# x^T of the fourth chunk by way of memory, and a first load without a fill in front of it

## The chip, the cores and the metric

The kernel runs on one core of one Trainium2 chip. A core has five engines that each work through a queue of their own: PE (TensorE, matmul), DVE (VectorE), ACT (ScalarE), POOL (GpSimd) and SP (SyncE), which here issues every DMA. Engines wait for each other by semaphores. The metric is the device time of one launch in microseconds (us). The kernel before takes 489.73 us, the median of 4 runs (489.62 to 489.83).

## The reference

Two blocks follow each other, all in fp32. The first is a gated recurrence over 4 batches x 8 heads, with sequence 768 and head size 48:

```
f = 1 / (1 + exp(-f_logit))
for t in range(S):
    state = f[t] * state + outer(k[t], v[t])      # per batch and head, 48 x 48
    y[t] = q[t] @ state
```

The outputs y are laid side by side by head as x, 3072 tokens x 384. The second block is a multiplicative feed-forward: `a = x @ w1`, `b = x @ w2`, `h = (a * b) @ w3`, `out = h @ w_out`, with 1024 inner columns. The weights come as 64-bit floats and are turned into fp32 on the chip.

## The kernel before

The 3072 tokens are cut into 24 chunks of 128 (NU = 24; u is the chunk, six per batch). A chunk of the recurrence is done as a small attention. Its gates come from f_logit by a sigmoid on ACT (L385), a forward scan and a backward scan over the gates on DVE (L393, L415) give the factors by which q and k are scaled (L409, L424), and PE makes the products inside the chunk (`pairs`), turns K (`turn`), applies the values (`values`), adds what the state gives (`from_state`) and updates the state (`update`). q, k and f of a chunk lie in tiles of 112 partitions: one head of each pair in partitions 0 to 47, the other in 64 to 111. Partitions 48 to 63 are a gap, which `setup` fills (30.0 for f, 0.0 for q and k): it fills partitions 32 to 63, and the loads then overwrite 32 to 47. So the first load of each such tile waits for its fill. In the kernel before all these fills are on POOL.

Four chunks make a block of 512 tokens (n is the block, NB = 6). The feed-forward wants x transposed, xt, in a tile of 128 x 3 x 512. How the y of a chunk gets there depends on the chunk:

- For u below NPE (= 4), PE does it: ACT brings y from PSUM (L663), six matmuls with a permutation (`moved`, L692) turn it, and ACT copies the result into xt (`settled`, L697).
- For the others, SP writes ys to a scratch tensor yt in memory (`written`, L684, two DMAs of 96 KB) and reads it back in its new order (`gathered`, L687, one DMA of 192 KB).

The constant NPE also chooses other things for the first four chunks, such as how the products are laid out in PSUM.

In block 0 the feed-forward is plain. `part(0, 2)` multiplies the tokens of chunks 0 and 1 by the first half of w1 and w2: four groups for a, then four for b, each of three fp32 matmuls of 256 columns. `part(2, 4)` does the same for chunks 2 and 3, then come groups of 512 columns for the second half of the weights. All are at L714, from the helper `three`. ACT takes each a out of PSUM (L751) and DVE multiplies b onto it (L756). Four PSUM banks serve the groups. From block 1 on the products are done with seven multiplications in place of eight (Strassen's way, in Winograd's form).

Beside that the weights are prepared. For each piece, ACT makes two passes over the 64-bit words (L1112, L1115), and DVE four (L1118, L1119, L1123, L1129). w3 and w_out are folded into one matrix on PE (L1176, eight folds), each fold as soon as its piece of w3 is done.

The order of instructions on each engine is made when the kernel is built: the class `Plan` lists tasks with an estimated cost, priorities and dependencies, and always takes the task that can start first. Engines then run that order strictly, and only waits shift it in time. A task that is removed or gets another cost therefore moves its neighbours on all engines, SP's queue among them. In the built program each DMA has one of eight completion semaphores in turn, and so a DMA is issued only after the one eight places before it has landed.

Of the kernel before, what the change touches and what calls it, by code (L numbers as in the profile page):

```python
# [44 lines left out]
B, H, S, D = 4, 8, 768, 48  # L45
# [13 lines left out]
NLEAF = 6  # L59
NQ = HP * C  # L60
NPE = 4
NRAW = 3
NF = 4
DH = DM // 2
# [125 lines left out]
def rows(par):  # L190
    return slice(64 * par, 64 * par + D)


def heads_of(u):

    return range(HP) if u < NPE else (0, 2, 1, 3)


def side(u, hp, par):

    if u < NPE:
        return par, hp
# [4 lines left out]
def ranged(ctx, tc, q, k, f_logit, v, w1, w2, w3, w_out, out, ident, w12, wc, left):  # L207

    nc = tc.nc
# [17 lines left out]
    qs, ks, fs = ([keep.tile([R, NQ], F32, name=f"{nm}{i}") for i in range(n)] for nm, n in (("q", 3), ("k", 2), ("f", 2)))  # L227
# [10 lines left out]
    def at(a, *shape):  # L238
        n = 1
        for m in shape:  # L240
            n *= m
        t = place[:, a : a + n]
        return t.rearrange("p (a b) -> p a b", a=shape[0]) if len(shape) == 2 else t
# [37 lines left out]
    def heads(t):  # L281
        return t.rearrange("p (h c) -> p h c", c=C)

    def setup():
        nc.scalar.activation(warm, nc.const_aps.tensor(0.0, (R, 1), F32), AF.Sigmoid)
        for i in range(2):
            nc.gpsimd.memset(fs[i][32:64], 30.0)
            nc.gpsimd.memset(ks[i][32:64], 0.0)
            nc.gpsimd.memset(qs[i][32:64], 0.0)
            if i == 0:  # L290
                make_identity(nc, ident)
        nc.gpsimd.memset(early[32:64, 2:4], 30.0)
        nc.gpsimd.memset(early[32:64, 0:2], 0.0)
        nc.gpsimd.memset(qs[2][32:64], 0.0)
        nc.gpsimd.memset(qs[3][32:64], 0.0)
        nc.vector.memset(floor, FLOOR)
        nc.vector.memset(heads(floor)[:, :, 0], 1.0)
        nc.vector.memset(back, 0.0)
        for t in gate:
            nc.vector.memset(t[:, NQ : NQ + 1], 0.0)  # L300
        for t in sb:
            nc.vector.memset(t, 0.0)

        nc.gpsimd.memset(perm, 0.0)
        for i, (kc, hp) in enumerate(met):
            for par in range(2):
                for r, t, at_, n in runs(2 * hp + par):
                    if t == kc:
                        a = 64 * par + at_
                        nc.gpsimd.tensor_copy(perm[:, i, r : r + n], ident[0:R, a : a + n])  # L310

    def runs(h):

        at_ = 0
        while at_ < D:
            t, r = divmod(h * D + at_, P)
            n = min(D - at_, P - r)
            yield r, t, at_, n
            at_ += n
# [7 lines left out]
    def need(u):  # L327
        return (0.0, 1.0, 2.0, 3.0)[u] if u < 4 else 60 + 14.5 * (u - 4)

    def past(u, n, *names):  # L330
        return [tk[u - n][nm] for nm in names if u >= n and nm in tk[u - n]]

    def moves(n, size, rate, emit, deps, prio, late=0.0):


        for j in range(n):
            i = plan.add("SP", 0.45, (lambda: None) if j else emit, [d] if j else deps, prio - j * 1e-3, takes=["lane"], lag=0.6)
            d = i
            t = plan.add("DMA", size / n / rate, lambda: None, [i], prio - j * 1e-3, lag=1.3 + late, frees=[i])
        return t  # L340

    def loaded(dst, u):

        if u < NPE:
            nc.sync.dma_start(dst, v[u])
# [6 lines left out]
    def front(u):  # L352

        s, t = st[u], tk[u]
        n0 = need(u)

        def load(dst, src):
            def emit():
                for par in range(2):
                    nc.sync.dma_start(dst[rows(par)], src[u, par])  # L360
            return emit

        fu, qu, ku = (x[u if u < 4 else u % n] for x, n in ((fs, 2), (qs, 3), (ks, 2)))

        def free(n, *names):

            if u < 4:
                return []
            return asked[8:9] + [tk[u - n if u - n >= 4 else u % n][nm] for nm in names]

        t["lf"] = moves(2, 197, 250, load(fu, f_logit), free(2, "g"), n0 - 30)
        t["lk"] = moves(2, 197, 250, load(ku, k), free(2, "k"), n0 - 29.5)
        t["lq"] = moves(2, 197, 250, load(qu, q), free(3, "q"), n0 - 29)

        def load_v():
            s["v"] = at(12288 + NQ, DM) if u == 3 else loads.tile([P, DM], F32, name="vt")
            loaded(s["v"], u)

        t["lv"] = moves(
            1 if u < NPE else 3, 197, 320, load_v, [] if u == 3 else past(u, 4 if u in (4, 5, 6) else 3, "v", "s"),  # L380
            n0 - (28.2, 28.2, 28.2, 29.6, 12)[min(u, NPE)],
        )

        def gates():
            nc.scalar.activation(gate[u % 2][:, 0:NQ], fu, AF.Sigmoid)  # L385

        t["g"] = plan.add("ACT", 0.65, gates, [t["lf"]] + past(u, 2, "r") + past(u, 3, "d"), n0)
        if u % NCH and "d" in tk[u - 1]:
            tk[u - 1]["d"]["deps"].append(t["g"])

        def forward():
            s["P"] = one.tile([R, NQ], F32, name="fwd")
            nc.vector.tensor_tensor_scan(s["P"], gate[u % 2][:, 0:NQ], floor, 0.0, ALU.mult, ALU.max)  # L393

        t["p"] = plan.add("DVE", 1.25, forward, [t["g"]] + past(u, 1, "q", "i", "l"), n0)

        def last():
            nc.scalar.copy(lasts[:, u], heads(s["P"])[:, :, C - 1])

        t["l"] = plan.add("ACT", 0.2, last, [t["p"]], n0)  # L400

        def ends():
            nc.vector.reciprocal(heads(back)[:, :, C - 1], heads(s["P"])[:, :, C - 1])

        t["i"] = plan.add("DVE", 0.18, ends, [t["p"]] + past(u, 1, "r"), n0)

        def scale_q():
            s["Q"] = work3.tile([R, NQ], F32, name="Q")
            nc.vector.tensor_tensor(s["Q"], qu, s["P"], ALU.mult)  # L409

        t["q"] = plan.add("DVE", 0.7, scale_q, [t["p"], t["lq"]] + past(u, 3, "v", "a"), n0 + 0.1)

        def backward():
            s["R"] = one.tile([R, NQ], F32, name="bwd")
            nc.vector.tensor_tensor_scan(  # L415
                s["R"][:, ::-1], gate[u % 2][:, NQ:0:-1], back[:, ::-1], 0.0, ALU.mult, ALU.max
            )

        t["r"] = plan.add("DVE", 1.25, backward, [t["i"]] + past(u, 1, "k"), n0)

        def scale_k():
            s["K"] = work.tile([R, NQ], F32, name="K")
            if u < NPE:
                nc.vector.tensor_tensor(s["K"], ku, s["R"], ALU.mult)  # L424
                return

            kk, k_, r_ = (
                x.rearrange("p (b two h c) -> p b two h c", two=2, h=2, c=C // 2) for x in (s["K"], ku, s["R"])
            )
            nc.vector.tensor_tensor(kk[:, :, 0], k_[:, :, 0], r_[:, :, 0], ALU.mult)  # L430
            nc.vector.tensor_tensor(kk[:, :, 1, ::-1], k_[:, :, 1], r_[:, :, 1], ALU.mult)

        t["k"] = plan.add("DVE", 0.7 if u < NPE else 0.8, scale_k, [t["r"], t["lk"]] + past(u, 2, "a", "t"), n0)
        if u in (2, 3):
            t["k"]["frees"].append(coming)
# [152 lines left out]
    def rest(u):  # L588
        s, t = st[u], tk[u]
# [81 lines left out]
        n = u // UB  # L671
# [7 lines left out]
        def written():  # L679

            s["yt"] = dram.tile([DM, C], F32, name="yt")
            for half in range(2):
                to = s["yt"][half * DH : half * DH + DH].rearrange("(b d) c -> d b c", d=D)
                nc.sync.dma_start(to, s["ys"][rows(half)])  # L684

        def gathered():
            nc.sync.dma_start(block_xt()[:, :, cols], s["yt"].rearrange("(k p) c -> p k c", p=P))  # L687
# [9 lines left out]
            nc.scalar.copy(block_xt()[:, :, cols], s["px"])  # L697

        before = blk[n - 2]["up"] if n >= 2 else []
        if u < NPE:  # L700
            t["z"] = plan.add("PE", 1.6, moved, [t["y"]], n0 - 996, takes=["f"], frees=[moving])
            t["x"] = plan.add("ACT", 0.55, settled, [t["z"]] + before, n0 - 20, frees=[t["z"]])
        else:
            t["z"] = moves(2, 197, 250, written, [t["y"]], n0 - 100)
            t["x"] = moves(1, 197, 250, gathered, [t["z"]] + before, n0 - 100)
# [358 lines left out]
    def fetch(loads_, a, prio, subs, deps=()):  # L1064
# [20 lines left out]
        else:  # L1085
            where = 2048 * ((load_no + 1) % NRAW)
        raw = at(where, 2 * total).bitcast(U32)
# [61 lines left out]
    def weights():  # L1149
# [60 lines left out]

        ready = [x for p in parts[-NRAW:] for x in p] + [x for p in pieces.values() for x in p]
        for which in range(2):
# [40 lines left out]
    def decided():  # L1253
        least = work.tile([1, 1], F32, name="least")
        nc.vector.tensor_reduce(out=least, in_=where["row"], axis=AX.X, op=ALU.min)
        nc.vector.tensor_scalar(left, least, 0.5, None, ALU.is_lt)

    setup()
    for u in range(NU):
        if u <= NPE:  # L1260
# [16 lines left out]
    for t in plan.order():  # L1277
        if t["eng"] == "PE" and t["at"] < FULL:
            n = int((t["at"] - ready_at) / 0.43)
# [343 lines left out]
```

## Time and profile before

| | |
|---|---|
| median of 4 runs | 489.73 us |
| the profiled execution | 489.78 us, of which the span of the instructions is 488.0 us |
| PE busy | 477.9 us (98%) |
| DVE busy | 359.8 us (74%) |
| ACT busy | 165.8 us (34%) |
| POOL busy | 61.5 us (13%) |
| mean granted TensorE clock | 0.997 |

Times in the trace count from the start of the span. A line such as "36.60 0.93 SPq L360 ..." is an entry of the timeline: start, duration, engine (SPq is SP's queue, where DMAs are issued), source line, operation, output and input; x2 is the number of instructions, and a bracket tells how long the engine was idle before it and what ended the idle time. An fp32 matmul leaves two records, so the 6 matmuls of `moved` are x12. Chunk u = 3 is the fourth. In what follows f4 stands for the load of f of chunk u = 4, and k4, q4, f5 and so on likewise.

### The profile page before, as it was taken

Reading aid. Unit: us, or ns where it says so; the run is one execution under the profiler, and the core shown is the slowest. Engines: PE = TensorE matmul, PEld = TensorE weight load, DVE = VectorE, ACT = ScalarE, POOL = GpSimd, SP = SyncE. Lnnn points to the kernel's source line nnn. Section 1 sums busy time; section 2 is a strip of 40 time slices with the busy share of each in tenths; the row PEclk is TensorE's granted clock in tenths of the full one; section 3 lists DMA queues with packets and bytes.
Section 4 is the critical chain, followed back from the end, with each engine's and each line's share of the span. In section 5 each row is a group of like instructions: output and inputs, shape, how many; then the busy total and the mean of one; then the engine's idle time right before and its main releaser. Section 6 shows DMA issues by size and latency. Waiting matters only on the chain.

```text
span 488.0 us, 9560 instructions
## 1 busy us (share of the span) xinstructions
PE 477.9 (98%) x3696; PEld 408.6 (84%) x3696; DVE 359.8 (74%) x721; ACT 165.8 (34%) x380; POOL 61.5 (13%) x115
## 2 busy tenths in 40 slices
PE   8899999999999999999999999999999999999995
PEld 6788744666799888899988888998899888889995
DVE  7999899999997688689877867456663667664541
ACT  3688456573334442544433441001100110110000
POOL 9210000305203111221311201000000000000000
PEclk9999999999999999999999999999999999999998
DMA  5999377663325654356642103000021000000011
GB/s 174 301 340 252 103 248 250 215 184 82 80 80 153 178 131 112 80 133 168 159 129 55 34 19 98 32 34 0 8 60 50 16 1 0 1 1 0 34 64 42
DMA packets 44920, 50.00 MB, mean 102 GB/s; under 512 B 15426, under 2 KB 34370, under 8 KB 43842
## 3 DMA queue, kind: packets, MB, share of 16 engines
q1 hardware_dynamic: 44866, 49.30, 34.6%
q8 instruction: 31, 0.51, 0.4%
q14 instruction: 23, 0.19, 0.1%
HBM read 40.63 MB, written 8.65 MB: 101 GB/s over the span
## 4 chain that ended last, share of the span: by engine, by line
PE 86%; DVE 6%; issue 1%; DVEq 0%
PE f L714 69%; PE f L1176 4%; PE py L490 4%; PE pa L456 2%; PE py L509 2%; PE py L468 2%; DVE place L1208 1%; PE f L523 1%; DVE place L1123 1%; DVE place L1129 1%; DVE bwd L415 1%; PE f L692 1%; DVE fwd L393 1%; DVE place L1222 0%; DVE place L950 0%
## 5 line engine op out<-in xcount | busy, mean ns | idle before, releaser
L714 PE MATMUL f<-xt,w 128*128 128x256 f32 (+1 forms) x600 | 159.0, 396 | 0.0
L714 PEld LDWEIGHTS f<-xt,w 128*128 128x128 f32 x600 | 113.5, 190 | 24.7 <-issue 11.0
L714 PE MATMUL f<-place 128*128 128x192 f32 (+1 forms) x504 | 112.5, 350 | 0.3 <-DVE place L950 0.3
L714 PEld LDWEIGHTS f<-place 128*128 128x128 f32 x504 | 87.9, 190 | 6.4 <-DVE place L950 0.6
L549 POOL TENSOR_SCALAR_AFFINE_SELECT A<-A 64x256 f32<-64x256 f32 (+1 forms) x84 | 49.0, 604 | 232.1 <-PE py L468 106.1
L1176 PE MATMUL f<-place 128*128 128x384 f32 x128 | 42.6, 489 | 0.5 <-DVE place L1129 0.5
L817 ACT COPY a<-f 128x256 f32<-128x256 f32 x36 | 13.4, 372 | 81.5 <-PE f L714 69.5
L1176 PEld LDWEIGHTS f<-place 128*128 128x128 f32 x128 | 23.9, 190 | 17.3 <-DVE place L1129 1.1
L714 PE MATMUL f<-xt,place 128*128 128x256 f32 x144 | 37.1, 380 | 0.0
L714 PE MATMUL f<-wc,ab 128*128 128x192 f32 x192 | 35.1, 326 | 0.0
L714 PEld LDWEIGHTS f<-wc,ab 128*128 128x128 f32 x192 | 32.0, 190 | 0.4
L393 DVE TENSOR_TENSOR_SCAN fwd<-gate,floor 112x512 f32<-112x512 f32 x24 | 29.8, 1243 | 2.6 <-ACT gate L385 2.1
L543 ACT COPY A<-pa 64x256 f32<-64x256 f32 (+1 forms) x60 | 24.2, 439 | 20.3 <-PE pa L456 19.6
L415 DVE TENSOR_TENSOR_SCAN bwd<-gate,back 112x512 f32<-112x512 f32 x24 | 29.6, 1234 | 0.7
L714 PEld LDWEIGHTS f<-xt,place 128*128 128x128 f32 x144 | 26.6, 189 | 3.5 <-DVE place L784 0.2
L841 DVE TENSOR_TENSOR place<-f,a 128x256 f32<-128x256 f32 x36 | 15.1, 421 | 18.8 <-PE f L714 18.5
L653 ACT COPY sb<-S 48x192 f32<-48x192 f32 x40 | 14.0, 350 | 27.9 <-DVE S L644 18.8
L490 PEld LDWEIGHTS py<-A,vt 128*64 128x64 f32 (+1 forms) x320 | 17.5, 129 | 6.7 <-issue 6.2
L490 PE MATMUL py<-A,vt 128*64 128x128 f32 x320 | 22.6, 281 | 0.0
L1112 ACT ACTIVATE place<-place 128x512 f32<-128x512 f32 (+2 forms) x24 | 21.2, 885 | 4.1 <-DVE w L1129 2.0
L714 PE MATMUL f<-place,w 128*128 128x256 f32 x72 | 21.4, 379 | 0.0
L1115 ACT ACTIVATE place<-place 128x512 f32<-128x512 uint32 (+2 forms) x24 | 21.3, 891 | 0.0
(119 smaller groups left out, 633.7 us busy)
## 6 DMA issues: line engine op xcount, KB each, us to landing
place<-in_w_dram SPq DMA_DIRECT2D x8, 1024.0 KB, 4.8
place<-in_w_dram SPq DMA_DIRECT2D x12, 512.0 KB, 9.0
out_dram<-o SPq DMA_DIRECT2D x24, 192.0 KB, 2.1
q<-in_q_dram SPq DMA_DIRECT2D x46, 96.0 KB, 2.4
f<-in_f_logit_dram SPq DMA_DIRECT2D x44, 96.0 KB, 2.3
k<-in_k_dram SPq DMA_DIRECT2D x44, 96.0 KB, 2.4
yt<-ys SPq DMA_DIRECT2D x40, 96.0 KB, 2.1
xt<-yt SPq DMA_DIRECT2D x20, 192.0 KB, 2.7
```

Source lines behind the costliest of these rows:

```text
L393: nc.vector.tensor_tensor_scan(s["P"], gate[u % 2][:, 0:NQ], floor, 0.0, ALU.mult, ALU.max)
L415: nc.vector.tensor_tensor_scan(s["R"][:, ::-1], gate[u % 2][:, NQ:0:-1], back[:, ::-1], 0.0, ALU.mult, ALU.max)
L490: nc.tensor.matmul(y_block(u, b)[64 * half : 64 * half + w], lhsT=s["v"][:, h * D : h * D + w], rhs=s["A"][:, par, hp], start=zone not in ...
L543: nc.scalar.copy(parts_of(s["A"].rearrange("p r h c -> p (r h c)"))[p0:p1, :, f], parts_of(s["pa"].rearrange("p r n -> p (r n)"))[p0:p1, : ...
L549: nc.gpsimd.affine_select(out=a, in_=a, pattern=pattern, compare_op=ALU.is_ge, fill=0.0, base=0, channel_multiplier=-1,)
L653: nc.scalar.copy(sb[u % 2][rows(par), :, 64 * par : 64 * par + D], s["S"][rows(par)])
L714: nc.tensor.matmul(out_, lhsT=lhs[i], rhs=rhs[i], start=start and i == 0, stop=i == len(lhs) - 1, skip_group_check=True,)
L817: nc.scalar.copy(q["a"], q["X"])
L841: nc.vector.tensor_tensor(ups["u3", k], q["Y"], q["a"], ALU.add)
L1112: nc.scalar.activation(m, hi.bitcast(F32), AF.Abs)
L1115: nc.scalar.activation(lo.bitcast(F32), lo, AF.Copy, bias=2.0, scale=2.0**-51)
L1176: nc.tensor.matmul(w3s["p", jc], lhsT=w3s[jc][:, kc * P : kc * P + P], rhs=wos[:, kc], start=(kc == 0), stop=(kc == KF - 1),)
```

## The change

The transposition of the fourth chunk (u = 3) goes by way of memory. A new constant NX = 3 takes NPE's place in the one test that chooses between the two ways, and `written` knows the layout that ys has in the first four chunks. The other part is in the start: the first load of f writes partitions 0 to 63 with one DMA of 64 rows, the last 16 of which are rows of the other head, and then partitions 64 to 111 as before. So f's first tile needs no fill. The fills of k and q of the second tiles move from POOL to DVE, behind the fills of `gate` and ahead of those of `sb`.

```diff
+NX = 3
...
         for i in range(2):
-            nc.gpsimd.memset(fs[i][32:64], 30.0)
-            nc.gpsimd.memset(ks[i][32:64], 0.0)
-            nc.gpsimd.memset(qs[i][32:64], 0.0)
             if i == 0:
+                nc.gpsimd.memset(ks[i][32:64], 0.0)
+                nc.gpsimd.memset(qs[i][32:64], 0.0)
                 make_identity(nc, ident)
+            else:
+                nc.gpsimd.memset(fs[i][32:64], 30.0)
...
             nc.vector.memset(t[:, NQ : NQ + 1], 0.0)
+        nc.vector.memset(ks[1][32:64], 0.0)
+        nc.vector.memset(qs[1][32:64], 0.0)
         for t in sb:
...
             def emit():
+                if dst is fs[0] and u == 0:
+
+                    nc.sync.dma_start(dst[0:64], src[u].rearrange("two d n -> (two d) n")[0:64])
+                    nc.sync.dma_start(dst[rows(1)], src[u, 1])
+                    return
                 for par in range(2):
...
             s["yt"] = dram.tile([DM, C], F32, name="yt")
+            heads_ = s["yt"].rearrange("(b p d) c -> d p b c", p=2, d=D)
             for half in range(2):
                 to = s["yt"][half * DH : half * DH + DH].rearrange("(b d) c -> d b c", d=D)
-                nc.sync.dma_start(to, s["ys"][rows(half)])
+                nc.sync.dma_start(heads_[:, half] if u < NPE else to, s["ys"][rows(half)])
...
-        if u < NPE:
+        if u < NX:
             t["z"] = plan.add("PE", 1.6, moved, [t["y"]], n0 - 996, takes=["f"], frees=[moving])
             t["x"] = plan.add("ACT", 0.55, settled, [t["z"]] + before, n0 - 20, frees=[t["z"]])
```

## The prediction

> **What bounds the kernel now.** I read the page first: PE is busy for 477.9 of 488.0 us. Then the chain of work that ended last, in order of time (start, duration, engine, tile, line):
>
> ```profile
> 34.30 1.53 PE f L692 x12
> 35.83 41.34 PE f L714 x144
> ...
> 77.26 0.69 DVE ab L756
> ...
> 81.56 1.24 DVE place L1129
> ...
> 82.84 5.43 PE f L1176 x16
> ```
>
> The 1.53 us are the six matmuls of the fourth chunk, and they lie on the chain. PE then runs without a gap to 77.2, DVE leads to 82.84, PE to 107.4, DVE to 135.1, PE to the end. A shift at 82.84 therefore reaches the end: fold 4 at 107.4 frees the buffer that DVE's next piece (L1123, 107.48) waits for. DVE is nearly as full as PE; the waits between 36 and 78 us are
>
> ```profile
> DVE ab L756 <- PE f L714: 2.0, 5, 0.8
> ```
>
> Then the timeline of the start:
>
> ```profile
> 0.81 0.52 POOL L287 MEMSET f<- 32x512 f32 x1 [0.29 <-POOLq L1610]
> ...
> 1.36 0.87 SPq L360 DMA_DIRECT2D f<-in_f_logit_dram  x2
> ...
> 4.24 0.63 ACT L385 ACTIVATE gate<-f 112x512 f32<-112x512 f32 x1 [1.93 <-DMA f<-in_f_logit_dram]
> ...
> 4.90 1.23 DVE L393 TENSOR_TENSOR_SCAN fwd<-gate,floor 112x512 f32<-112x512 f32 x1 [1.79 <-ACT gate L385]
> ```
>
> The first load waits for the fill, the gate for the load, the scan for the gate; DVE then has no wait over 0.1 us until 29.65 (0.6). Last, SP's queue and the DMAs where the new transfers fall:
>
> ```profile
> 33.74 0.37 SPq L1093 DMA_DIRECT2D place<-in_w_dram  x1
> 34.16 0.90 SPq L360 DMA_DIRECT2D k<-in_k_dram  x2
> 35.10 0.89 SPq L360 DMA_DIRECT2D q<-in_q_dram  x2
> 36.16 0.40 SPq L1093 DMA_DIRECT2D place<-in_w_out_dram  x1
> 36.60 0.93 SPq L360 DMA_DIRECT2D f<-in_f_logit_dram  x2
> ```
>
> and, for the second f5 DMA, issued at 37.06, the DMA answer of the window 37 to 37.6 (last number: us from issue to landing):
>
> ```profile
> f<-in_f_logit_dram SPq DMA_DIRECT2D x2, 96.0 KB, 8.3
> ```
>
> 8.3 us, where the same size lands in 2.3 us in the median of all: a backlog. By stretches of 2 us from 36 to 46 the DMA share is 0.99 to 1.06, and it is 0.9 or more from about 17 us on. The landings in that stretch come in the order of issue: w 39.14, k4 39.4 to 39.8, q4 39.9 to 40.4, w_out 44.66, f5 44.9 to 45.4.
>
> **What the skill says.** The Trainium skill, "DMA: Bandwidth & Descriptors", section "Queues, rings and completion order": SP's DMAs share one row of rings, and each DMA engine takes descriptors in ring order. The landings above agree: a late DMA can't pass the backlog. Section "Anatomy of one DMA" of that page, written for the path by GpSimd, puts a fixed cost near 2 us on a DMA, most of it the receipt; on SP's path here the shortest yt or xt takes 1.9 us. "TensorE: Matmul & The Clock Gate", Part 1, says that the clock halves after an idle window of about 3.4 us; no wait of PE here is that long, and even its first idle us shows clock 1.00.
>
> **The start.** The first DMA can go when SP is released, at 0.82, in place of 1.36: 0.54 us. It brings 32 KB more, 0.1 us at the 269 GB/s of the first 30 us. The gate comes at about 3.75 and the scan at 4.4. DVE gets two fills of 0.48 us (the floor row of this width), and was free from 3.12; now from 4.1, so 0.3 us of cover is left, and each us beyond would delay the scan by as much. SP comes to k1 at 4.6, after its fill (3.1). POOL loses three fills and delays nobody. SP issues its first 28 DMAs 0.47 us apart, so the queue shifts too. Worth: 0.5 us on DVE and PE, about 0.4 us in the DMA backlog. Between nothing (if SP is released later than I read) and 0.54; I take 0.5. Without more, PE's `values` at 30.22 comes at 29.7.
>
> **The matmuls.** 1.53 us go, so PE's first group at L714 starts at 33.7 in place of 35.75. Its weights are there: the third w1 piece (L1129, done 33.56) now at 33.1; the last w2 piece (39.93) at 39.4, for a matmul due at 39.9. The eight groups of part(0, 2) take 1.29 us each (ACT's and DVE's takings are that far apart), so part(2, 4), which needs the fourth chunk, could start at 44.06 in place of 46.1. ACT loses its copy of 0.48 us, off the path: it waits 11.7 us for L714 between 36 and 78.
>
> **The way through memory.** The built order on SP is now w, k4, yt, yt, w_out, q4, f5, xt, k5, w_out, q5. ys is ready (L663 ends at 33.46, now 33.0) before SP gets there at 34.6; the two writes then cost SP 0.9 us of issue. xt waits for them to land (about 39.5 to 40.5), and SP stands still till then with k5, w_out and q5 behind it; none is wanted before 50 us. So xt is issued at about 40.3, but its turn comes when all in front of it has landed: w, k4, w_out, q4, f5 as before (45.4), 0.4 earlier, plus yt and xt themselves. Their 768 packets of 512 B are 48 for each of 16 DMA engines. Two v loads in the same backlog (64 packets each engine) took from 32.8 to 34.9: 33 ns a packet, so 1.6 us. Four xt in a row later moved 786 KB in 3.2 us, 31 ns: 1.5 us. From both sides: at the best rate shown (421 GB/s) 384 KB take 0.9 us; at the rate of w_out (768 KB in 4.26 us) 2.1. I take 1.6. xt lands at 45.4 - 0.4 + 1.6 = 46.6, and PE resumes at 46.65: it waits 2.6 us, and is 0.55 later than the 46.1 of before. More than both gains is lost in that wait.
>
> **The order on DVE.** The planner has moved several L756 one place forward, ahead of a weight pass, so DVE waits for PE more often. The first in part(2, 4) comes before an L1129 and waits 1.5 us; DVE's former waits (2.0) take that up. Near the end the third wide L756 now precedes L1129: before it started at 72.36, with its product ready at 72.1; now the product comes at 72.65, and after it follow 0.61 for itself, 0.88 for that L1129 and 3.71 for the four passes of the next piece. So the last L756 starts at 77.85 in place of 77.26 (+0.59), and L403, now behind it, adds 0.18 ahead of the passes that fold 1 waits for. Fold 1 starts at 83.6 in place of 82.84: +0.77.
>
> **Sum.** 489.78 + 0.77 = 490.55 for the profiled execution; the median lies 0.05 lower: 490.5 us. Every 0.1 us of xt's landing moves this by 0.1; the break-even is a landing at 45.8.
>
> **Rivals.** *In time.* If the small transfers slip through, by DMA engines that run ahead of the slowest, xt lands by 44.1 and both gains stay: PE is 2.0 us early, DVE follows to 80.85 (its waits of 2.0 vanish, 0.2 stays for the order): -1.8, 487.9 us. For it: the first us of PE saved are on the chain. Against: f5, issued a little earlier, landed at 45.4. From 45.8 down it decides for a gain. *Dearer transfers.* If writes to memory in 512-byte packets cost double in the backlog, 3.2 us in place of 1.6, xt lands at 48.2, the wait passes the 3.4 us of the clock window, and the time is 492.1, or up to 493 with a slower clock. *No gain at the start*, since SP isn't released at 0.82, or the fills on DVE delay the scan: the backlog then shifts by nothing or is 0.1 later, and xt lands at 47.0 to 47.1: 490.9.
>
> **How the numbers follow.** Forecast: 0.70, own range 489.4 to 491.5 (0.9 to 2.1 us for the transfers, and up to half a us on either side for the backlog). In time: 0.12. Dearer: 0.12. No gain at the start: 0.06. About 0.2%, 1 us, is what a measurement can tell here. The forecast case lies within 0.2% for 0.42 and above for 0.28; with the rivals that makes faster 0.12, same 0.44, slower 0.44. The range leaves out half of the two outer rivals: 488.6 to 492.1.
>
> **What would show it.** The first load issued near 0.85 and the first scan at about 4.4; `values` near 29.7; L714 starting near 33.7; xt issued near 40.3 and landing 6 us later; then one wait of PE for that DMA of about 2.6 us at 44.1, where before there was none; the first L756 after it waiting about 1.5; fold 1 at 83.6. A landing of xt under 4 us from its issue, a second yt landing long after 41, or fold 1 before 82 would each show me wrong.

## The result, and the profile after

The changed kernel takes 490.95 us (median of 34 executions, 489.34 to 495.96), the kernel before, measured beside it, 489.78 us (489.29 to 490.73). The ratio is 1.0035 (95% interval 1.0025 to 1.0044): the change costs 1.2 us by the medians and 1.7 by the ratio, which the long executions weigh on. In the profiled execution of the changed kernel the time is 490.31 us and the span 488.6 us, against 489.78 and 488.0 us before; its granted clock is 0.998.

Lines of the changed kernel have moved by 9 or 10: L724 is the former L714, L766 the former L756, L1186 the former L1176, L1133 and L1139 the former L1123 and L1129, L394 and L402 the former L385 and L393; L694 and L697 are the new transfers of yt and xt. The experiments below move lines by up to four more; the tile names stay.

The page's costliest group of the changed kernel (busy time, mean ns, then idle time ahead of it and what ended most of it) has a wait that it didn't have before:

```profile
L724 PE MATMUL f<-xt,w 128*128 128x256 f32 (+1 forms) x600 | 159.4, 396 | 1.5 <-DMA xt<-yt 1.5
```

The chain that ended last, of the changed kernel (start, duration, what):

```profile
34.02 1.51 PE f L724 x6
...
36.34 4.27 DMA yt<-ys
40.68 5.29 DMA xt<-yt
46.10 28.64 PE f L724 x90
...
77.46 0.68 DVE ab L766
...
81.96 1.24 DVE place L1139
83.24 5.43 PE f L1186 x16
```

PE's matmuls at 34.30 to 35.83 are gone and its feed-forward starts at 33.95 in place of 35.67 (the chain shows its first piece from 34.02), but the chain now leaves PE for the two transfers: yt is written in 4.3 us, xt read in 5.3, and PE goes on at 46.10. The prediction had put the same group at 46.1 in the kernel before, so everything that PE had won is spent in the wait of 1.5 us. From there the path leads through DVE as before, and fold 1 starts at 83.24 in place of 82.84, 0.40 later, although PE went on no later than before. DVE's new order is the likely reason; no run here changes that order alone. PE and DVE between 34 and 80 us, by their waits (in total, times, longest):

```profile
DVE ab L766 <- PE f L724: 3.3, 3, 1.8
...
PE f L724 <- DMA xt<-yt: 1.5, 1, 1.5
```

The start of the changed kernel, in its timeline:

```profile
0.82 0.59 SPq L365 DMA_DIRECT2D f<-in_f_logit_dram  x1
...
1.46 0.56 SPq L366 DMA_DIRECT2D f<-in_f_logit_dram  x1
...
3.95 0.63 ACT L394 ACTIVATE gate<-f 112x512 f32<-112x512 f32 x1 [1.64 <-DMA f<-in_f_logit_dram]
...
4.62 1.23 DVE L402 TENSOR_TENSOR_SCAN fwd<-gate,floor 112x512 f32<-112x512 f32 x1 [0.23 <-ACT gate L394]
```

The load goes 0.54 us sooner, but gate and scan come only 0.29 and 0.28 sooner. And SP's queue where the new transfers fall, in the timeline of the changed kernel:

```profile
32.11 0.34 SPq L1103 DMA_DIRECT2D place<-in_w_dram  x1
...
34.52 0.37 SPq L1103 DMA_DIRECT2D place<-in_w_dram  x1
...
35.92 0.86 SPq L694 DMA_DIRECT2D yt<-ys  x2
...
40.68 0.39 SPq L697 DMA_DIRECT2D xt<-yt  x1
```

The first of these lines matters most for what follows. It is the last w load but one, and SP can issue it only when an earlier load has landed. In the profiled execution of the kernel before it was issued at 31.07; here, in spite of the earlier start, at 32.11.

The 34 times aren't one heap. With two more executions and the 20 of the second measurement below, 56 executions of the changed kernel are on record, each with its mean granted clock. In 36 of them the time is 491.81 us or less, with a clock of 0.996 or more and a median near 490.6 us. The other 20 take 491.99 to 495.96 us, and in 18 of those the clock is 0.990 to 0.994. Beside them the kernel before stays within 489.23 and 490.73. So there were two things to explain: a typical loss of about 0.8 us, and a loss of two to six in a third of the executions.

The mean clock is a coarse sign. It also counts what comes after PE's last matmul: in the profile of the kernel before the clock is 0.50 from 484.57 to the end, and the mean 0.997. A clock of one half for 3.4 us in mid-kernel costs the mean about 0.0035. So a mean of 0.996 or 0.997 can hide such a stretch, as the profile of the way through memory alone shows below (0.996). None of the 111 executions of the kernel before whose clock is listed has a mean below 0.996, so 0.994 or less tells of one.

### The profile page after: what moved, and what is told of

Read it like the earlier page. It is cut to its first block, busy times and chain, and to the rows that moved or that the text cites. A ratio compares the mean times of both kernels' runs of the same rounds, so it can differ in the third digit from the quotient of the medians.

```text
span 488.6 us, 9538 instructions
## 1 busy us (share of the span) xinstructions
PE 476.2 (97%) x3684; PEld 406.5 (83%) x3684; DVE 360.1 (74%) x723; ACT 164.9 (34%) x379; POOL 60.9 (12%) x112
## 4 chain that ended last, share of the span: by engine, by line
PE 83%; DVE 6%; DMA 2%; issue 1%; ACT 1%; SPq 0%; ACTq 0%; DVEq 0%
PE f L724 67%; PE f L1186 4%; PE py L499 4%; PE pa L465 2%; PE py L518 2%; PE py L477 2%; DVE place L1218 1%; PE f L532 1%; DMA xt<-yt 1%; DMA yt<-ys 1%; DVE bwd L424 1%; DVE place L1133 1%; DVE place L1139 1%; DVE fwd L402 1%; DVE place L1232 0%
## 5 line engine op out<-in xcount | busy, mean ns | idle before, releaser
L724 PE MATMUL f<-xt,w 128*128 128x256 f32 (+1 forms) x600 | 159.4, 396 | 1.5 <-DMA xt<-yt 1.5
L724 PEld LDWEIGHTS f<-xt,w 128*128 128x128 f32 x600 | 113.4, 190 | 26.6 <-issue 10.5
L724 PE MATMUL f<-place 128*128 128x192 f32 (+1 forms) x504 | 112.5, 350 | 0.3 <-DVE place L960 0.3
L724 PEld LDWEIGHTS f<-place 128*128 128x128 f32 x504 | 87.9, 190 | 6.4 <-DVE place L960 0.6
L1186 PE MATMUL f<-place 128*128 128x384 f32 x128 | 42.7, 489 | 0.5 <-ACT place L1125 0.3
L1186 PEld LDWEIGHTS f<-place 128*128 128x128 f32 x128 | 23.8, 190 | 17.6 <-ACT place L1125 1.1
L724 PE MATMUL f<-xt,place 128*128 128x256 f32 x144 | 37.1, 380 | 0.0
L724 PE MATMUL f<-wc,ab 128*128 128x192 f32 x192 | 35.1, 326 | 0.0
L724 PEld LDWEIGHTS f<-wc,ab 128*128 128x128 f32 x192 | 32.0, 190 | 0.4
L402 DVE TENSOR_TENSOR_SCAN fwd<-gate,floor 112x512 f32<-112x512 f32 x24 | 29.8, 1243 | 1.0 <-ACT gate L394 0.5
L424 DVE TENSOR_TENSOR_SCAN bwd<-gate,back 112x512 f32<-112x512 f32 x24 | 29.7, 1236 | 0.8
L724 PEld LDWEIGHTS f<-xt,place 128*128 128x128 f32 x144 | 26.6, 189 | 3.5 <-issue 0.2
L724 PE MATMUL f<-place,w 128*128 128x256 f32 x72 | 21.4, 379 | 0.0
```

Of the source, the lines that this page charges most:

```text
L424: nc.vector.tensor_tensor_scan(s["R"][:, ::-1], gate[u % 2][:, NQ:0:-1], back[:, ::-1], 0.0, ALU.mult, ALU.max)
L724: nc.tensor.matmul(out_, lhsT=lhs[i], rhs=rhs[i], start=start and i == 0, stop=i == len(lhs) - 1, skip_group_check=True,)
L1186: nc.tensor.matmul(w3s["p", jc], lhsT=w3s[jc][:, kc * P : kc * P + P], rhs=wos[:, kc], start=(kc == 0), stop=(kc == KF - 1),)
```

## The experiments

Theory: the loss is PE's wait for xt, and xt lands when the bytes asked for before it have been moved. The rivals to it: xt's place in SP's queue and not the bytes; the round trip through memory itself; the order on DVE, which the planner changed too; and for the long executions, PE's clock after the wait.

**The changed kernel once more**, without an edit, to see how much of the profile is the kernel and how much the execution.

> The changed kernel once more, for a second sample of the landing of xt. Theory 1 (the prediction's: xt stands in SP's backlog and PE waits for it, and nothing else is lost): PE's one wait for xt between 1 and 3 us, and the time is 488.8 + that wait, within 0.4, at a clock of 0.996 or more. Theory 2 (the wait also lets the clock of PE fall in a part of the executions): the executions fall into two groups, one near 490.5 with clock 0.996 to 1.0 and one at 492 to 496 with clock 0.990 to 0.995, as the listed clocks of the first result suggest.

Measured: 491.4 us (20 executions, 489.97 to 495.74), ratio 1.0041 (1.0025 to 1.0058); 9 of the 20 had a clock of 0.991 to 0.994 and took 492.13 us or more. This time the profiled execution (494.93 us, clock 0.991) is one of those. Its xt was issued at 42.30 and landed at 47.5, and PE waited 3.3 us. By stretches of its span (length, busy time and instructions of PE, PEld, DVE, ACT and POOL, then PE's granted clock, DMA share and GB/s), cut where the clock changes:

```profile
43.57:46.98 3.41, 0.79 (x4) 0.36 (x2) 2.21 (x8) 2.16 (x5) 0.00 (x0) 1.00 1.03 190
46.98:50.39 3.41, 2.73 (x7) 2.22 (x8) 1.27 (x4) 0.39 (x1) 0.00 (x0) 0.50 0.99 303
50.39:53.81 3.42, 3.42 (x10) 2.70 (x9) 0.59 (x2) 1.49 (x4) 0.00 (x0) 0.50 0.99 195
53.81:57.22 3.41, 3.41 (x17) 3.02 (x16) 2.81 (x7) 1.30 (x2) 0.00 (x0) 1.00 0.04 9
```

The clock is 0.50 from 46.98 to 53.81: PE is busy all through 50.39 to 53.81 us and gets 10 matmul records done where it does 17 in the next stretch of that length. The same 90 records of L724 that took 28.64 us from 46.10 on take 31.67 here. One half of 6.83 us is 3.4 us, and 3.0 of it falls on these records. So the wait is paid twice, once as a wait and once in the matmuls behind it.

**The start alone**, and later a second time with more executions.

```diff
-NX = 3
+NX = 4
```

> Only the start is changed (first load without a fill, two fills on DVE); the fourth chunk is turned on PE as before. Theory: the 0.28 us by which the first scan came earlier in the changed kernel goes to the end: 489.5, executions within 0.5 us of each other. Rival: it is lost where PE waits for DVE or for weights, 489.8.

> The start's part of the change alone, on another chip, with more executions. Theory (the start is worth the 0.3 us by which the first scan and `values` came earlier in the profile of the changed kernel): 0.2 to 0.4 us below the kernel before, ratio 0.9992 to 0.9996. Rival (nothing of it reaches the end): ratio 1.0000 to within 0.0003.

Measured: 489.54 us (12 executions) beside 489.89, ratio 0.9993 (0.9984 to 1.0002); then 489.57 us (13 executions) beside 489.75, ratio 0.9997 (0.9989 to 1.0005). Both medians lie below the kernel before, by 0.35 and 0.18 us, and neither interval leaves out 1. The chain of the second profiled execution:

```profile
34.11 1.53 PE f L702 x12
35.65 41.34 PE f L724 x144
...
82.66 5.43 PE f L1186 x16
```

The six matmuls are back, PE runs for 41.34 us without a gap as in the kernel before, and fold 1 starts 0.18 us sooner than there (0.54 sooner in the first one). No execution of the 25 had a clock under 0.996. The start is worth 0.2 to 0.5 us in the trace, and what the change loses is all in the fourth chunk.

**The way through memory alone**: the kernel before with `NX = 3` and the new `written`, its start as it was.

```diff
+NX = 3
...
-                nc.sync.dma_start(to, s["ys"][rows(half)])
+                nc.sync.dma_start(heads_[:, half] if u < NPE else to, s["ys"][rows(half)])
...
-        if u < NPE:
+        if u < NX:
```

> Only the way through memory; the start is as before. Theory 1: the median is 0.3 us above that of the changed kernel (about 491.2), with one wait of PE for xt of 1.5 to 2 us. If the start mattered for when xt lands, the wait is the same and everything is 0.3 later; if not, the wait is 0.3 shorter and the median the same as that of the changed kernel.

Measured: 492.77 us (7 executions, 489.59 to 494.71), ratio 1.0048 (1.0018 to 1.0078), above the 491.2 expected. The profiled execution, 494.71 us, issued xt at 43.78; it landed at 48.4, and PE waited 4.0 us, with a clock of 0.57 in the stretch from 48 to 52 us. The spread of 5 us comes with this part and not with the start. Seven executions with such a spread don't say whether the start moves xt.

**The transfers by another queue**: yt and xt of the fourth chunk issued by GpSimd.

```diff
-                nc.sync.dma_start(heads_[:, half] if u < NPE else to, s["ys"][rows(half)])
+                (nc.gpsimd if u < NPE else nc.sync).dma_start(heads_[:, half] if u < NPE else to, s["ys"][rows(half)])
...
-            nc.sync.dma_start(block_xt()[:, :, cols], s["yt"].rearrange("(k p) c -> p k c", p=P))
+            (nc.gpsimd if u < NPE else nc.sync).dma_start(block_xt()[:, :, cols], s["yt"].rearrange("(k p) c -> p k c", p=P))
```

> The changed kernel, with the two writes of yt and the read of xt for the fourth chunk issued by GpSimd, in place of SP. Theory 1 (the place in SP's ring is what delays xt): xt lands before 43, PE doesn't wait for it, fold 1 starts at 81 to 82, 488.0 to 488.5, and no execution with a low clock. Rival (the DMA engines are full whatever the queue): xt lands at 45 to 46 again, PE waits 1 us or more, 490.0 to 490.6.

Measured: 490.69 us (11 executions, 489.87 to 493.4), ratio 1.0031 (1.0015 to 1.0048), in effect the changed kernel's. GpSimd issues yt at 33.48 and xt at 38.59, both about 2 us sooner than SP had, but xt takes 7.8 us from there and lands at 46.4. A queue of its own didn't lead past the backlog here. The Trainium skill, "DMA: Bandwidth & Descriptors", section "Queues, rings and completion order", says that each DMA engine goes round between the rows that it has work for, packet by packet. This run doesn't show such turns at once: from 38.6 to 42.8 us the trace has 507 packets of SP's queue and none of GpSimd's, and all 64 of GpSimd's move between 42.8 and 45.5. Why they began 4.3 us after the issue isn't shown, and GpSimd's transfers also come in larger packets (2 and 4 KB in the trace, SP's yt and xt 512 B). So the run shows that another queue didn't help, and not whether the order in SP's ring or the capacity of the DMA engines is what delays xt. It also shows a halved clock after a wait of only 2.0 us:

```profile
44.00:48.00 4.00, 2.03 (x7) 1.39 (x6) 3.24 (x9) 2.31 (x4) 0.00 (x0) 0.84 1.03 265
48.00:52.00 4.00, 4.00 (x15) 3.32 (x15) 0.86 (x2) 1.49 (x4) 0.00 (x0) 0.74 0.83 183
```

**More bytes ahead of xt**: ys is also written to two spare tensors just before yt, 384 KB in 768 packets.

```diff
+EXTRA = 2
...
+            for i in range(EXTRA if u == 3 else 0):
+                spare = dram.tile([DM, C], F32, name=f"spare{i}").rearrange("(b p d) c -> d p b c", p=2, d=D)
+                for half in range(2):
+                    nc.sync.dma_start(spare[:, half], s["ys"][rows(half)])
```

> The changed kernel with ys written to two spare tensors as well, ahead of yt: 384 KB more, in 768 packets of 512 B. Theory 1: at the 31 to 33 ns a packet and DMA engine of the prediction xt lands 1.5 us later, at 47.5 to 50. Theory 2: the wait is then 3 us or more in most executions, so most have the low clock as well, and the median is 493.5 to 495. If transfers of this kind cost nothing in the backlog: 491, as the changed kernel.

Measured: 493.86 us (6 executions, 492.6 to 497.36), ratio 1.0093 (1.0062 to 1.0123). In the profiled execution xt was issued at 42.87 and landed at 48.3, 2.3 us after the landing in the first profile of the changed kernel, and PE waited 4.0 us; both lie where the theory put them (47.5 to 50, and 3 us or more).

**All of the backlog behind xt**: w_out, q4 and everything of chunks 5 and 6 wait in the planner for yt's task, of which xt comes next.

```diff
-            return asked[8:9] + [tk[u - n if u - n >= 4 else u % n][nm] for nm in names]
+            late = [tk[3]["x"]["deps"][0]] if u in (5, 6) or (u == 4 and names == ("q",)) else []
+            return late + asked[8:9] + [tk[u - n if u - n >= 4 else u % n][nm] for nm in names]
...
-        held = holders(where, 2 * total)
+        held = holders(where, 2 * total) + ([tk[3]["x"]["deps"][0]] if load_no == 12 else [])
```

(The v load of chunk 6 is held in the same way.)

> The changed kernel with SP's queue in another order: the loads of w_out, q4 and all loads of chunks 5 and 6 come behind the read of xt, so that xt follows the two yt writes at once. Theory 1 (what stands in front of xt in SP's ring is what delays it): xt is issued when yt has landed (40.3 to 42.3), lands 2.5 to 3 us later, at 43 to 45, PE waits 0 to 0.7 us, no execution at a low clock, 488.2 to 489.0. Rival (it is late whatever stands in front, since the writes are): PE waits 1.5 us or more and the time is that of the changed kernel.

Measured: 492.82 us (5 executions), ratio 1.0067 (1.0043 to 1.0091): slower than the changed kernel, against the 488.2 to 489.0 expected, and with a mean clock of 0.993 and 0.994 in two of the five. xt takes 2.6 us from its issue at 42.05 and lands at 44.7, and PE waits 0.4 us for it, as expected. The waits of that execution from 34 to 80 us show what is late in its place:

```profile
ACT place L1126 <- DMA place<-in_w_out_dram: 5.6, 2, 3.3
DVE ab L767 <- ACT ab L762: 4.8, 2, 3.1
```

ACT works through its list in order. It comes to its passes over w_out, which hasn't landed, and the copies of a behind them wait with them. DVE waits for those copies, and so does PE, 1.6 us at 52.8. The DMA engines weren't at their limit: their share is 0.05 from 41 to 42 us and 0.00 from 42 to 43. Everything else stood in SP's queue behind xt, and xt stood there till yt had landed, so the engines had nothing to move. Here the planner also put two DVE passes and a gate on ACT elsewhere, and the run doesn't tell what that adds.

**The clock by itself**: four idle matmuls on PE, on data that is already there, just ahead of the first group that needs xt. They fill the wait with work of no use.

```diff
+WARM = 4
...
                 def emit():
+                    if n == 0 and c0 == 2 and jc == 0 and which == 0:
+                        idle(WARM)
                     s["pu", jc, which, c0] = bank()
```

> The changed kernel with four matmuls on constants (256 columns, thrown away) on PE in front of the first group that needs xt. Theory 2 (the wait lets the clock fall): PE is busy for 1.9 us of the wait, what remains of the wait is 0 to 2 us, the executions at 0.990 to 0.995 go, the slowest is under 492.5 and the median is 490.5. Without the clock (theory 1 alone): the same median as the changed kernel, 491, and still some at 493 to 496.

Measured: 490.87 us (13 executions, 490.19 to 492.36), ratio 1.0028 (1.0019 to 1.0036). The mean clock is 0.997 or more in all 13, where it was 0.990 to 0.994 in 18 of 56 without the filler, and no execution passes 492.36, where 17 of the 56 did. (The run with more bytes ahead of xt, measured beside this one, has 0.990 to 0.994 in 3 of 6.) What makes the longest executions long is thus in part PE's clock after the wait; the rest of it is the longer wait itself, 3.3 us in place of 1.5 in the second profile of the changed kernel. A mean of 0.997, which the two longest of the 13 have, doesn't rule out a short fall in them. The typical loss stays, and isn't the clock: xt landed at 45.5 in the profiled execution, fold 1 started at 83.29, and the fillers take as long as the wait did.

**Part of the backlog behind xt**: only q4 and f5, 384 KB, are put behind xt; w, k4 and the first w_out piece keep their places. The order on PE, DVE and ACT is that of the changed kernel to the instruction, and on SP only these loads change places with xt (and k5 with the second w_out piece behind it). The edit is the one with `late` above, without the last line of that diff.

> The changed kernel with q4 and f5 (384 KB) put behind xt on SP; w, k4 and the first w_out piece stay ahead of it, and the order on PE, DVE and ACT is that of the changed kernel to the instruction. Theory (backlog: xt ends when the bytes asked for before it have been moved): xt, which landed at 46.0 and 47.5 in the two profiles of the changed kernel, lands 1.0 to 1.5 us earlier, at about 45.2 (44.5 to 46.2); PE waits 0.3 to 1.5 us for it; w_out still lands near 44, so ACT isn't held up; 489.7 us (489.2 to 490.3), and executions with a clock under 0.995 all but vanish, since the wait is shorter. Rival (the round trip itself: yt's landing and then some 5 us for xt, whatever else is queued): xt still lands at 46 to 47.5 and the time stays at 490.9 to 491.4.

Measured: 489.0 us (14 executions, 488.31 to 491.13) beside 489.75 us, ratio 0.9989 (0.998 to 0.9997). This beats the kernel before by 0.75 us (0.5 by the ratio), and lies about 1.9 us below the changed kernel, which was measured at another time. It is also below the 489.2 to 490.3 expected. The clock is 0.997 or more in all 14. The chain of its profiled execution (488.31 us):

```profile
33.77 38.96 PE f L725 x138
...
81.23 5.43 PE f L1187 x16
```

PE runs from 33.77 on without a wait for xt. xt was issued at 40.66, as in the changed kernel, but it took 3.1 us in place of 5.3:

```profile
L698 SPq DMA_DIRECT2D xt<-yt x1: 377/377/377, 40.7 to 40.7; - x1
...
DMA to landing us min/median/max: 3.1/3.1/3.1
```

It landed at 43.8, earlier than I expected (44.5 to 46.2). The rival, that the round trip takes its 5 us whatever is queued, falls. Two of the 14 took 490.21 and 491.13 us at a full clock; no profile shows what was late in those.

**k4 behind xt as well**, another 192 KB, the same edit with `names` of k for chunk 4.

> As the run before, with k4 (192 KB) put behind xt too, so that only w and w_out1 stay ahead of it; ACT has its pass over w_out and the gate of chunk 4 exchanged for one place. Theory (backlog): xt lands about 0.6 us earlier again, 44.6 (44 to 45.5), PE waits under 1 us for it, 489.3 us (488.8 to 490.0). What would then be late is w_out or nothing. Rival (round trip): no earlier than 46, 490.9 or more.

Measured: 489.78 us (12 executions, 488.27 to 493.35), ratio 1.0001 (0.9987 to 1.0016). xt landed at 45.1 for 44.6 expected, and again took 3.1 us from its issue, so holding back k4 too didn't shorten the read. In the profiled execution w_out is late once more and DVE waits 2.7 us for ACT. Here ACT's pass over w_out also stands elsewhere in its order, so this run doesn't say whether the loss against the run before is the order's or the execution's.

**No transposition of the fourth chunk at all**, its columns of xt filled with a constant on GpSimd, to see the most that the change could bring. In the first form the tasks are taken out of the plan, in the second they stay in it and only their instructions are left out, so that PE, DVE and ACT keep the changed kernel's order.

```diff
+            if u == NX:
+                t["x"] = plan.add("POOL", 0.5, lambda: nc.gpsimd.memset(block_xt()[:, :, cols], 0.5), before, n0 - 100)
+                return
             t["z"] = moves(2, 197, 250, written, [t["y"]], n0 - 100)
```

> The changed kernel without any transposition of the fourth chunk: its columns of xt are filled with a constant by GpSimd early on (part of the computation is left out, the output for these tokens is not computed). It gives the most that the change could bring. Theory (the wait for xt is what the change pays): the 1.53 us of matmuls and the 0.3 us of the start are both gained, no wait of PE between 36 and 60 us: 488.1 us (487.6 to 488.7). Rival (the order on DVE or the weights would have held PE back anyway): 489.3 or more, with waits of PE for w or for a buffer in the place of xt.

Measured: 491.52 us (10 executions, 489.81 to 492.08), ratio 1.0031 (1.0021 to 1.0041): no gain at all, against my expectation. The chain of its profiled execution:

```profile
34.01 38.96 PE f L727 x138
...
74.63 1.06 ACT place L1128
75.70 1.86 issue
77.56 12.25 PE f L1189 x32
```

PE has its 2 us in hand at 72.97, as it should. Then it waits 2.0 us ahead of fold 0. The chain names no releaser there ("issue"), but DVE's last pass over the piece of w3 that fold 0 reads runs from 76.24 to 77.46, and the fold starts at 77.56: the planner had put DVE's work in another order. And behind that wait stands the halved clock, so that the two folds take 12.25 us where two of 5.43 are usual:

```profile
76.00:80.00 4.00, 2.44 (x4) 1.50 (x5) 3.93 (x6) 1.16 (x2) 0.00 (x0) 0.70 0.74 283
80.00:84.00 4.00, 4.00 (x12) 2.26 (x11) 3.97 (x7) 1.59 (x2) 0.00 (x0) 0.88 0.52 154
```

The second form settles whether it was the order or the early PE as such:

```diff
         def written():
-
+            if u == NX:
+                return
             s["yt"] = dram.tile([DM, C], F32, name="yt")
...
         def gathered():
+            if u == NX:
+                nc.gpsimd.memset(block_xt()[:, :, cols], 0.5)
+                return
```

> The changed kernel with the order of every instruction on PE, DVE and ACT as it is, but the three transfers of the fourth chunk left out and its columns of xt filled with a constant by GpSimd (part of the computation is left out; the output for these tokens is not computed). It separates the two readings of the run without the fourth chunk, where the planner had also put another order on DVE and ACT. Theory (that run lost its gain to the order: fold 0 found its w3 piece late and waited 2.0 us, the clock halved after it): here no such wait and no wait for xt, fold 1 at 81.0 to 81.4 us, 488.2 us (487.8 to 488.7), about as the run with q4 and f5 behind xt, and no execution with a clock under 0.995. Rival (a PE that is 2 us early runs into the unfinished w3 piece in any order): a wait of 1 us or more at fold 0, fold 1 at 82.5 or later, 489.5 us or more.

Measured: 488.25 us (7 executions, 487.89 to 488.72) beside 489.78, ratio 0.9968 (0.9957 to 0.998), clock 0.996 or more in all. So it was the order. The profiled execution is the longest of the seven, and its fold 1 starts at 81.75, later than expected, for a reason that bears on everything above:

```profile
24.21 11.66 DMA place<-in_w_dram
35.89 0.33 SPq L369
...
38.20 8.34 DMA place<-in_w_out_dram
```

One w load of 512 KB took 11.7 us, and SP issued f4 and what follows only when it had landed. The first w_out piece then landed at 46.5. ACT waited 2.0 us for it, and the gate behind that pass came so late that DVE waited 2.0 us for the gate.

**The landings side by side.** The profiled executions, sorted by what was queued ahead of xt; times in us from the start of the span. The second column is the issue of the last w load but one, which stands ahead of all these edits in SP's order; only the start's part of the change comes before it.

| kernel | that w load issued | xt issued | xt landed | landed less w issued | PE waits for xt |
|---|---|---|---|---|---|
| 384 KB more | 31.71 | 42.87 | 48.3 | 16.6 | 4.0 |
| changed | 32.11 | 40.68 | 46.0 | 13.9 | 1.5 |
| changed again | 32.52 | 42.30 | 47.5 | 15.0 | 3.3 |
| memory alone | 34.16 | 43.78 | 48.4 | 14.2 | 4.0 |
| by GpSimd | 32.67 | 38.59 | 46.4 | 13.7 | 2.0 |
| idle matmuls | 31.45 | 39.91 | 45.5 | 14.1 | none |
| q4, f5 behind | 31.77 | 40.66 | 43.8 | 12.0 | none |
| q4, f5, k4 behind | 33.47 | 41.95 | 45.1 | 11.6 | 0.8 |
| w_out, q4, f5 behind | 32.63 | 42.05 | 44.7 | 12.1 | 0.4 |

Three things come out of it. With the changed kernel's bytes ahead, xt lands 13.7 to 15.0 us after that w load; with 384 KB more 16.6, with 384 KB fewer 12.0. That is the backlog: some 2 us for 384 KB, in either direction (1.6 to 3.0 by these single profiles). Holding back still more brings little: 11.6 and 12.1. What is left there is yt's own way and the 2.6 to 3.1 us of the read. And the w load itself is issued anywhere between 31.45 and 34.16 in this table, and in all 14 profiled executions of this study between 31.07 and 34.41. Nine of these profiles are of kernels that do the same up to that load, and they differ by 3.0 us (31.45 to 34.41); the two kernels that were profiled twice differ by 0.4 and 0.2. The 31.07, the earliest of all, is that of the kernel before, from which the prediction was made.

**When a wait costs the clock.** The traces show it. In all 14 the clock keeps 1.00 or 0.50 for whole multiples of 3.41 us between two changes, as from 46.98 to 53.81 above, so each trace can be cut into windows of 3.41 us, counted forward and back from a change; the bounds between them are called marks here. Of 1967 windows at full clock 19 are followed by a fall, and PE was idle for 1.97 us or more in each of the 19. The other 1948 had 1.83 us of idle time or less, save one with 1.98. So what counts in these runs is the idle time inside one window, with the limit at about 2.0 of 3.41 us. In the second profile of the changed kernel 2.6 of the 3.3 us lie before the mark at 46.98 and 0.7 behind it: the clock falls at the mark and stays low for a second window. The waits of 4.0 us end within 0.04 us of a mark, PE is busy through the window behind it, and one window is all they cost. A wait of 1.6 us in the run with all of the backlog behind xt, 52.80 to 54.38, lies inside one window and costs nothing more.

## Why the prediction was right, and where not

**What bounds the kernel, and the sign: right.** The matmuls lay on the path, and without the fourth chunk's work in any form, in the same order, the time falls to 488.25 us. The wait for xt takes that gain back; with xt in time it returns (489.0 us). 490.5 us were forecast, 490.95 measured, and about 490.6 for the shorter 36 executions. That the median lies so near is in part luck: it is the middle of two groups, and of the second one, with the fallen clock, the forecast case says nothing.

**The start: mechanism right, size wrong.** I gave it 0.5 us, from the issue of the first load. The term left out is that the two new DMAs take longer to issue: 0.59 and 0.56 us, where the two of before took 0.87 together. The second of them is issued at 1.46 in place of about 1.81, and it is the one the gate waits for, 2.5 us later in either kernel. `values` came at 29.94 in place of 30.22: 0.28 us, and 29.7 was forecast. DVE's two fills did end before the gate, as predicted, and the scan still waited 0.23 us for it.

**The backlog 0.4 us sooner: wrong.** SP's queue didn't follow the start. It came to the last w load but one 1.0 us later than in the profile of before, and 1.4 in the second. That stretch varies by 3 us among the profiles, and in the kernel before nobody on the path waits for anything in it.

**The matmuls: right.** L724 started at 33.95 for 33.7 predicted, the difference being mostly the start's.

**xt's landing: near, as a sum of two errors.** 46.6 was predicted from 45.4 - 0.4 + 1.6; 46.0 and 47.5 were measured. xt's issue at 40.3 came out at 40.68 and 42.30, and "6 us later" as 5.3 and 5.2. The 1.6 us for 384 KB has its measured counterpart in the landings above, near 2. (The 786 KB in 3.2 us of that sum are 33 ns a packet, and not 31; the 1.6 stays.) That xt lands later with more in front of it, and sooner with less, agrees with the runs that moved bytes. That the engines' capacity is the reason, and not only the order of the queue, isn't shown.

**The wait: right in kind, 1.5 for 2.6 us in one profile and 3.3 in the other.** The step that failed is the sentence on the clock, "no wait of PE here is that long". The Trainium skill, "TensorE: Matmul & The Clock Gate", Part 1, says that the clock is cold after one idle window or more, of about 3.4 us, and that the window runs free of the kernel. I read it as a wait of 3.4 us. The traces show a halved clock after waits of 2.0, 2.0, 3.3, 4.0 and 4.0 us, and none after 0.4, 0.8, 1.5 and 1.6. The length of the window agrees with the page: the missing clock adds up to 1.7 us in four of the five, half of 3.4, and to twice that after the 3.3. But a window need not be idle throughout, 2.0 us of it were enough. The rival "dearer transfers" named this outcome, 492.1 or up to 493, and gave it 0.12; times of 491.99 us and more came in 20 of 56 executions and reached 495.96. In the profiled one of them, the backlog was late and the packets weren't dear: xt took 5.2 us from its issue, as in the other profile.

**The order on DVE: right in kind as far as shown.** I took 0.22 us for it beyond PE's delay of 0.55. The first L766 of part(2, 4) waited 1.8 us for 1.5 predicted. In the profile PE was not late at all against 46.1, and fold 1 still came 0.40 later. With xt in time PE is 2.0 us early and fold 1 1.61: 0.4 again. So the wait takes the gain away, and what the first profiled execution loses beyond that, 0.53 us, is near the order's 0.4; no run with the old order and xt in time was made. The runs without the fourth chunk show how much an order can cost, over 3 us between the two forms, of which the clock behind the wait is 1.7.

**The rivals.** "In time" needed small transfers to slip through; they didn't, but where loads were held back for them its time came near: 487.9 forecast, 488.31 in a profiled execution. "No gain at the start" is half true and would have given 490.9 for the wrong term.

## What to carry to other kernels

A transfer off the critical path has no reason to be on time, and one profile shows one draw of when it lands. Before work is made to wait for it, its landing has to be known as a spread over executions, and the reserve has to be larger than the spread. Another queue didn't help here; what helped was to hold back loads that nobody needed yet, and only those. Holding back more left the DMA engines idle and made another load late.

A wait of the tensor engine is priced with the clock behind it. Two microseconds could cost almost four here, and by the windows above a wait of this length should cost nothing more than itself when a mark divides it evenly, which no run here shows. So such a wait has no fixed price until it is well under 2 us.

Where a planner orders the work, an experiment that removes a task also shuffles the rest. Keeping the task in the plan and leaving out its instructions made the one run readable.

## What the runs showed of the hardware

- PE's clock stood at 1.00 or 0.50 for whole windows of 3.41 us. It fell behind a window with 1.97 us or more of idle time (19 of 19 falls in 14 traces), and didn't behind 1947 windows with 1.83 us or less; at 1.97 and 1.98 there is one window of either kind. One window at half clock with 0.7 us of idle time was followed by a second one; five with at most 0.04 us were followed by the full clock. With idle matmuls in the wait no mean clock of 13 was under 0.997.
- A transfer of 192 KB issued by GpSimd's queue, with the DMA engines at a share of about 0.9 or more, took 7.8 us, of which 4.3 passed before its first packet. SP's took 5.3, and 3.1 with 384 KB fewer in front.
- The issue of the last 512 KB w load but one, which waits for earlier landings, drifted by 3.0 us between nine profiles of kernels that do the same up to that point. They ran on several chips, but two on the same chip still lie 1.7 us apart (31.77 and 33.47). What makes one slower stays open.
